# Attention block with sliding window and gated FFN on one core: values of eight heads in one stretch, probabilities kept per two heads

## The chip, the cores and the metric

The kernel runs on one core of one Trainium2 chip. The metric is device time in microseconds (us) of one execution; the figure that counts is the median over runs. Engines are called as in the profile: PE (matrix engine; PEld its weight loads), DVE (vector), ACT (scalar), POOL (GpSimd), SP (the queue that issues most transfers).

## The reference, cut to what matters

One transformer block over 2048 tokens of width 640, in fp32: layer norm, attention with 32 heads of 20 over a causal window of 256 tokens, residual, layer norm, gated FFN of width 1536, residual.

```python
qkv = layernorm(x) @ wqkv                      # 32 heads of 20
scores = q @ k.T * 20 ** -0.5                  # kept where 0 <= query - key < 256
o = softmax(scores) @ v @ wo
h = x + o
out = h + (gelu(layernorm(h) @ w_gate) * (layernorm(h) @ w_up)) @ w_down
```

## The kernel before, in words

The tokens are cut into 16 blocks of 128. A block's queries see their own block of keys and the two before it (`window`, L812), so blocks 0 and 1 see one and two, all others three. The dense products (q, k, v, output projection, FFN) are done as two fp16 halves per operand, three matmuls per product (`products`, L540).

Attention of one block has three kinds of PE work, each in a mode of the array of its own:

* **Maxima** (`maxima`, L834): for one pair of heads, q times k in row tiles (60 of 64 rows per head), into the PSUM tile `ra` or `rb` (two banks each, one per head of the pair). DVE then adds the mask and takes the row maximum with one `tensor_tensor_reduce` per head (`max_out`, L906). In the profile this is a `CUSTOM_DVE_ANT_0` row and a short `DVE_READ_ACCUMULATOR2_ANT` row that writes the maximum to `mxs`. The reduce also writes its elementwise result, which nobody reads; before, that goes to an SBUF tile `junk`, of which there is one.
* **Scores** (`scores`, L951): once all maxima of a block are known, they are put beside q as two more rows, and k times q in row tiles gives the transposed scores less the maximum, into the other of `ra` and `rb`. ACT takes the exponential into the SBUF tile `pt`, and POOL sets masked probabilities to zero with `affine_select`: two calls for the far edge of the window and one for the diagonal, and the diagonal alone in blocks 0 and 1 (`score_out`, L989).
* **Values** (`value_lane`, L1016): probabilities times v, four heads at a time in four column tiles, fp32, into `pv`. A unit of four heads is 4 matmuls per key block: 12 in most blocks, 24 records in the trace, since an fp32 matmul leaves two.

Dense matmuls and transposes use the whole array. After every second value group of eight heads ACT copies `pv` out, and the result is transposed and normalised.

**What sets the order.** The kernel is written as Python generators ("lanes"). A planner (`Clock`, `Engine`, and the loop at the end of `block_kernel`) prices each instruction with a small formula and issues the first lane whose inputs are ready by its own clock. The order that results is fixed at build time; each engine runs its list in order and waits on semaphores. The planner prices a change of array mode at 0.095 us (`SWITCH`), a DVE op on 320 elements at 0.065 + 0.00106 x 320 = 0.404 us, and a hop between engines at 0.18 us (`LAT`). If a tile's ring of buffers is full, the new tile counts as written when its predecessor's last use ends, and the hop is added (`tile`, L126): with its one buffer, `junk` makes each reduce start 0.18 us after the one before it, in the planner's clock.

`row_need` (L860) says when a maxima or scores stretch may start: its banks have to be free, and for scores a place in the ring of `pt` as well (three units of four heads). The loop tries values ahead of all else when PE is in row mode (`nc.mode == "row"`, L1633), so that a value stretch follows a row stretch where it can; when fewer than two units wait (`len(valq) < 2`, L1635) values aren't started from any other mode.

While nothing is ready and no score has been computed yet, the loop issues a 128-column matmul on `ident16` into `pv`, to keep PE going ("warmers" below).

Of the kernel before, what the change touches and what calls it, by code (L numbers as in the profile page):

```python
# [22 lines left out]
P = 128  # L23
# [230 lines left out]
def block_kernel(ctx: ExitStack, tc: tile.TileContext, x, wqkv, wo, wg, wu, wd, out):  # L254
# [85 lines left out]
    nc.vector.tensor_copy(ident16, ident)  # L340
    mhalf = const.tile([P, 1], F32, name="mhalf")
    nc.vector.memset(mhalf, -0.5)
    ones = const.tile([P, P], F32, name="ones")
    nc.vector.memset(ones, 1.0)


    NS = 16
# [229 lines left out]
    def ff_scales_down(fg):  # L577
# [15 lines left out]
    gu = gu.rearrange("p (a c f) -> p a c f", c=KC, f=512)  # L593

    HB = P // 2
    mask = wp.tile([P, 2 * P], F32, name="mask")
    nc.gpsimd.memset(mask, 0.0)
    nc.gpsimd.affine_select(mask[:, P:2 * P], mask[:, P:2 * P], pattern=[[-1, P]],
                            compare_op=ALU.is_ge, fill=NEG, base=0, channel_multiplier=1)
    band = wp.tile([P, 5 * HB], F32, name="band")  # L600
    nc.gpsimd.memset(band, 0.0)
    for a in range(2):
        first, last = band[HB * a:HB * a + HB, 0:HB], band[HB * a:HB * a + HB, 4 * HB:]
# [5 lines left out]
    maxq, tps, scoreq, valq, woq = [], [], deque(), deque(), deque()  # L609


    RV, RK = 5, 6
    vring = [wp.tile([P, H, DH + 1], F32, name=f"v{i}") for i in range(RV)]
    rooms["v"] = [v.rearrange("p h d -> p (h d)")[:, :D] for v in vring]
    kT = wp.tile([P, H // 2, RK, P], F16, name="kT")
# [97 lines left out]

    def load_x(j):
        if 0 < j < NR:
            t = at("pt", [P, 4, 3, P], F32, 3).rearrange("p a b c -> p (a b c)")
            B[j].x = t[:, 0:D]
        else:
            B[j].x = at("xt", [P, D], F32)
        nc.sync.dma_start(B[j].x, x[j * P:(j + 1) * P, :])  # L720
# [94 lines left out]
    def pairs(j):  # L815

        return 2 if j < 2 else 1
# [42 lines left out]
    def row_need():  # L860


        (ta, a), (tb, b_) = sorted((two(n), n) for n in ("ra", "rb"))
        tm, ts = [], []
        lead = pos["max"] - pos["score"]
        for j, pr in heapq.nsmallest(2, maxq) if lead < 2 * LEAD else ():
            b = B[j]
            tm.append(nc.ready((b.c.qT[0:60, pr, b.cols], kT[0:60, pr, j % RK, :],
                                b.c.qT[64:124, pr, b.cols], kT[64:124, pr, j % RK, :]),
                               "tensor"))  # L870
        free = 3 - (pos["units"] - pos["values"])
        for j, pr in list(scoreq)[:2]:
            b = B[j]
            free -= pr % 2 == 0
            if free >= 0:
                ts.append(nc.ready((b.c.qT[0:62, pr, b.cols], b.c.qT[64:126, pr, b.cols]),
                                   "tensor"))
        row.clear()
        late = max(ta, nc.t["tensor"]) + APART
        two_of = [(maxima, scores, tm[:1] + ts[:1]), (scores, scores, ts), (maxima, maxima, tm)]  # L880
        if lead > LEAD + SWAY:
            two_of = [two_of[1], two_of[0], two_of[2]]
        elif lead < LEAD - SWAY:
# [12 lines left out]
        return one[0][0]  # L896
# [9 lines left out]
    def max_out(j, pr, par, ps, at_):  # L906
        b = B[j]
        n = len(window(j))
        for k in range(pairs(j)):
            w = min(n * P, 5 * HB)  # L910
            head = ps[:, k * n * P:k * n * P + w]
            yield on("vector", head)
            junk = at("junk", [P, 5 * HB], BF16, 1)
            nc.vector.tensor_tensor_reduce(junk[:, :w], head,
                                           band if n == 3 else mask[:, (2 - n) * P:], 1.0,
                                           -3.0e38, ALU.add, ALU.max,
                                           b.mx[:, par * 16 + pr + k:par * 16 + pr + k + 1])
        done(at_)
        b.maxima += pairs(j)
        if b.maxima == H:  # L920
            tps.append(max_rows(j))
# [29 lines left out]
    def scores(at_):  # L951
        j, pr = scoreq.popleft()
        b = B[j]
        u = pr // 2
        if pr % 2 == 0:
            b.pt[u] = at("pt", [P, 4, 3, P], F32, 3)
            pos["units"] += 1
        n = len(window(j))
        t = bank(at_).rearrange("p (r c) -> p r c", r=2)
        for k in range(pairs(j)):  # L960
            if n == 3:
                steps = [((1, slice(0, 2), 1, 3),) * 2,
                         ((2, slice(0, 2), 3, 5), (0, slice(0, 2), 0, 6)),
                         ((0, slice(0, 1), 0, 1), (2, slice(1, 2), 4, 5))]
# [13 lines left out]
        t = t[:, :, :pairs(j) * n * P]  # L978
        tasks.append(score_out(j, pr, t, b.pt[u], at_))
        pos["score"] += pairs(j)  # L980

    def part(pt, n, i):
# [3 lines left out]
            return half[:, :, 2 * i:2 * i + 2]  # L986
        return (half[:, :, 0:6:5], half[:, :, 1:3], half[:, :, 3:5])[i]

    def score_out(j, pr, t, pt, at_):  # L989
        b = B[j]  # L990
        u = pr // 2
        n = len(window(j))
        m = pairs(j)
        yield on("scalar", t)
        w = min(n * P, 5 * HB)
        for k in range(m):
            h = 2 * (pr % 2 + k)
            nc.scalar.activation(pt[:, h:h + 2].rearrange("p h a b -> p h (a b)")[:, :, :w],
                                 t[:, :, k * n * P:k * n * P + w], AF.Exp, scale=esc)
        done(at_)  # L1000
        pos[j, u] += 2 * m
        if pos[j, u] < 4:
            return
        yield on("gpsimd", pt[:, :, 0, :])
        if n == 3:
            half = pt.rearrange("p h a (b c) -> p h (a b) c", b=2)
            for a, (i, o) in enumerate(((0, 0), (3, 5))):
                nc.gpsimd.affine_select(half[:, :, o], half[:, :, i], pattern=[[0, 4], [-1, HB]],
                                        compare_op=ALU.is_ge, fill=0.0, base=-1 - HB * a,
                                        channel_multiplier=1)  # L1010
        diag = part(pt, n, n - 1).rearrange("p h a b -> p h (a b)")
        nc.gpsimd.affine_select(diag, diag, pattern=[[0, 4], [1, P]],
                                compare_op=ALU.is_ge, fill=0.0, base=0, channel_multiplier=-1)
        valq.append((j, u))

    def value_lane():  # L1016

        while True:
            yield pe(when=lambda: valq and B[valq[0][0]].v == 2 and pos["ones"])
            j, u = valq.popleft()  # L1020
            b = B[j]
            pt = b.pt.pop(u)
            ks = window(j)
            n = len(ks)
            order = [1, 0, 2] if n == 3 else list(range(n))
            yield pe(pt, pv[:, u % 4, :])
            for k, i in enumerate(order):
                for c in range(4):
                    nc.tensor.matmul(pv[32 * c:32 * c + DH + 1, u % 4, :].rearrange(
                                         "p (a b) -> p a b", b=HB),  # L1030
                                     vring[ks[i] % RV][:, 4 * u + c, :], part(pt, n, i)[:, c],
                                     start=(k == 0), stop=(k == n - 1))
            pos["values"] += 1
# [665 lines left out]
```

## Time and profile before

| | |
|---|---|
| median of 3 runs | 1014.98 us (1014.44 to 1020.82) |
| the profiled execution, its own time | 1018.26 us |
| its span, first to last instruction | 1016.5 us |
| PE busy | 998.2 us (98%), 12925 matmul records |
| DVE busy | 749.2 us (74%) |
| ACT busy | 446.6 us (44%) |
| POOL busy | 313.2 us (31%) |
| granted PE clock | 1.00 throughout |

The attention part runs from the first maxima stretch at 52.4 us to about 583 us; after that PE does the FFN alone. Busy time of PE is modelled and overlaps, so the distance from one matmul's start to the next one's is the cost that counts; the timeline shows starts, and merges equal neighbours into one row with a count (x4, x12, x24). A "stretch" below is an unbroken run of matmuls of one kind.

### The profile page before, as it was taken

How to read it: one execution, taken by the hardware profiler on the slowest of the kernel's cores; microseconds unless marked ns; L12 is line 12 of the kernel's file. 1: busy time of each engine (PE TensorE's matmuls, PEld its weight loads, DVE VectorE, ACT ScalarE, POOL GpSimd, SP SyncE). 2: the span in 40 equal slices, each digit the busy share in tenths (PEclk: the TensorE clock that was granted, in tenths of full speed). 3: DMA queues.
4: the chain of work that ended last, by engine and by line, in shares of the span. 5: the costliest groups of instructions: out<-in, count | busy, mean ns of one | idle time of the engine just before them, and what ended most of it. 6: DMA issues, size and time to landing. Idle time of an engine off the chain costs nothing.

```text
span 1016.5 us, 30774 instructions
## 1 busy us (share of the span) xinstructions
PE 998.2 (98%) x12925; PEld 699.3 (69%) x12925; DVE 749.2 (74%) x2206; ACT 446.6 (44%) x721; POOL 313.2 (31%) x504
## 2 busy tenths in 40 slices
PE   8999999999999999999999999999999999999998
PEld 7876666766766676777655664567777777777776
DVE  5888898888867767775687687798888875544553
ACT  6514856755555555554657643432222222221220
POOL 7101544543433433332435411254313300000000
PEclk9999999999999999999999999999999999999999
DMA  8657587361441614127103433233553442222211
GB/s 308 131 121 170 156 165 203 83 148 39 114 113 54 119 53 108 43 67 191 36 29 106 93 118 104 78 130 111 143 188 94 144 153 78 79 99 84 79 53 52
DMA packets 105835, 112.68 MB, mean 111 GB/s; under 512 B 38368, under 2 KB 79584, under 8 KB 105696
## 3 DMA queue, kind: packets, MB, share of 16 engines
q1 hardware_dynamic: 93600, 99.97, 36.0%
q10 hardware_dynamic: 12096, 10.75, 3.4%
q8 instruction: 101, 1.65, 0.7%
q14 instruction: 38, 0.31, 0.1%
HBM read 73.73 MB, written 28.84 MB: 101 GB/s over the span
## 4 chain that ended last, share of the span: by engine, by line
PE 82%; DVE 7%; DMA 5%; ACT 3%; POOL 2%; issue 2%; SPq 0%; ACTq 0%; DVEq 0%; POOLq 0%
PE mm L199 41%; PE ra L199 12%; PE pv L199 11%; PE rb L199 10%; PE tp L199 7%; DVE junk L199 1%; DMA wsl<-in_wu_dram 1%; DMA kT<-qk 1%; DMA qk<-qks 1%; POOL pt L199 1%; DVE am L199 1%; DMA qT<-in_wqkv_dram 1%; ACT pt L199 1%; DVE ht L199 1%; POOL gu L199 0%
## 5 line engine op out<-in xcount | busy, mean ns | idle before, releaser
L199 POOL TENSOR_SCALAR_AFFINE_SELECT pt<-pt 128x512 f32<-128x512 f32 x352 | 174.4, 511 | 300.8 <-ACT pt L199 284.9
L199 DVE CUSTOM_DVE_ANT_0 junk<-ra,band 128x320 bf16<-128x320 f32 x238 | 116.4, 489 | 50.5 <-PE ra L199 45.1
L199 ACT ACTIVATE pt<-rb,esc 128x640 f32<-128x640 f32 (+2 forms) x135 | 102.4, 765 | 81.6 <-PE rb L199 61.1
L199 DVE CUSTOM_DVE_ANT_0 junk<-rb,band 128x320 bf16<-128x320 f32 x210 | 102.8, 489 | 35.0 <-PE rb L199 29.7
L199 ACT ACTIVATE pt<-ra,esc 128x640 f32<-128x640 f32 (+2 forms) x121 | 92.2, 769 | 67.3 <-PE ra L199 59.1
L199 PE MATMUL pv<-pt,v 128*21 128x128 f32 x2880 | 104.5, 275 | 1.2 <-issue 1.1
L199 PEld LDWEIGHTS <-ah 128*128 128x128 f16 x768 | 75.1, 98 | 28.5 <-issue 1.2
L199 ACT ACTIVATE gel<-gel,ffk 128x512 f32<-128x512 f32 x36 | 26.0, 721 | 135.6 <-DVE gel L199 135.6
L199 PEld LDWEIGHTS <-ws 128*128 128x128 f16 x720 | 70.4, 98 | 9.2 <-DVE ws L199 1.1
L199 PEld LDWEIGHTS pv<-pt,v 128*21 128x21 f32 x2880 | 68.5, 100 | 10.2 <-issue 0.8
L199 PEld LDWEIGHTS <-kT 62*64 62x64 f16 x2880 | 63.8, 106 | 11.9 <-issue 7.6
L199 PEld LDWEIGHTS <-qT 60*64 60x64 f16 x1280 | 30.2, 104 | 58.9 <-issue 50.8
L199 PEld LDWEIGHTS <-gu 128*128 128x128 f16 x440 | 41.8, 98 | 36.2 <-issue 2.1
L199 DVE SCALAR_TENSOR_TENSOR ht<-mm,ffk,ht 128x320 f32<-128x320 f32 x96 | 52.2, 545 | 13.9 <-PE mm L199 12.1
L199 ACT CAST ah<-gel 128x512 f16<-128x512 f32 x48 | 29.6, 617 | 70.6 <-DVE gel L199 70.4
L199 PE MATMUL mm<-xh,w1h 128*128 128x256 f16 x200 | 54.7, 273 | 0.9 <-DVE qks L199 0.9
L199 PE MATMUL mm<-xl,w1h 128*128 128x256 f16 x200 | 54.7, 273 | 0.0
L199 PE MATMUL mm<-xh,w1l 128*128 128x256 f16 x200 | 54.7, 273 | 0.0
L199 POOL TENSOR_TENSOR gelt<-gelt 128x256 f32<-128x256 f32 x18 | 15.5, 859 | 112.6 <-ACT gelt L199 112.6
L199 PE MATMUL mm<-w3h,ol 128*128 128x320 f16 x160 | 48.1, 301 | 0.0
L199 PE MATMUL mm<-w2h,xl 128*128 128x320 f16 x160 | 48.1, 300 | 0.0
L199 PE MATMUL mm<-w3h,oh 128*128 128x320 f16 x160 | 48.0, 300 | 0.0
(300 smaller groups left out, 2576.9 us busy)
## 6 DMA issues: line engine op xcount, KB each, us to landing
ws<-wsums SPq DMA_DIRECT2D x24, 640.0 KB
qk<-qks ACTq DMA_DIRECT2D x32, 256.0 KB
qT<-qk SPq DMA_DIRECT2D x48, 160.0 KB
kT<-qk SPq DMA_DIRECT2D x48, 160.0 KB
wsums<-ws SPq DMA_DIRECT2D x12, 640.0 KB
ht<-in_x_dram SPq DMA_DIRECT2D x16, 320.0 KB
h_dram<-ht SPq DMA_DIRECT2D x16, 320.0 KB
ht<-h_dram SPq DMA_DIRECT2D x16, 320.0 KB
```

What stands on the lines that cost most here:

```text
L199: r = real(*args, **kw)
```

## The change

Five edits, in `block_kernel` and the functions printed above:

1. `value_lane` takes two units (eight heads) at once: it waits until two are queued and all four of their probability tiles and both quarters of `pv` are ready, and issues both without a break.
2. `pt` becomes a ring of seven tiles of two heads, where it was three tiles of four heads. `row_need` counts in these.
3. POOL masks each two-head tile by itself: the same three calls (or one) on half as many elements, so twice as many calls.
4. The reduce for the maxima writes its unread elementwise result back over its own input in PSUM; `junk` is gone.
5. `mask` and `band` become bf16, and the unused tile `ones` is dropped, to make room in SBUF.

The diff, cut to its core:

```diff
-    ones = const.tile([P, P], F32, name="ones")
-    nc.vector.memset(ones, 1.0)
...
-    mask = wp.tile([P, 2 * P], F32, name="mask")
+    mask = wp.tile([P, 2 * P], BF16, name="mask")
...
-    band = wp.tile([P, 5 * HB], F32, name="band")
+    band = wp.tile([P, 5 * HB], BF16, name="band")
...
-    RV, RK = 5, 6
+    RV, RK, RP = 5, 6, 7
...
-        free = 3 - (pos["units"] - pos["values"])
+        free = RP - (pos["parts"] - 2 * pos["values"])
...
-            free -= pr % 2 == 0
+            free -= pairs(j)
...
-            junk = at("junk", [P, 5 * HB], BF16, 1)
-            nc.vector.tensor_tensor_reduce(junk[:, :w], head,
+            nc.vector.tensor_tensor_reduce(head, head,
                                            band if n == 3 else mask[:, (2 - n) * P:], 1.0,
...
-        u = pr // 2
-        if pr % 2 == 0:
-            b.pt[u] = at("pt", [P, 4, 3, P], F32, 3)
-            pos["units"] += 1
+        for k in range(pairs(j)):
+            b.pt[pr + k] = at("pt", [P, 2, 3, P], F32, RP)
+        pos["parts"] += pairs(j)
...
+        for k in range(pr, pr + pairs(j)):
+            pt = b.pt[k]
+            yield on("gpsimd", pt[:, :, 0, :])
+            if n == 3:
+                half = pt.rearrange("p h a (b c) -> p h (a b) c", b=2)
+                for a, (i, o) in enumerate(((0, 0), (3, 5))):
+                    nc.gpsimd.affine_select(half[:, :, o], half[:, :, i],
+                                            pattern=[[0, 2], [-1, HB]], compare_op=ALU.is_ge,
+                                            fill=0.0, base=-1 - HB * a, channel_multiplier=1)
...
+            pos[j, "u", k // 2] += 1
+            if pos[j, "u", k // 2] == 2:
+                valq.append((j, k // 2))
...
-            yield pe(when=lambda: valq and B[valq[0][0]].v == 2 and pos["ones"])
-            j, u = valq.popleft()
+            yield pe(when=lambda: len(valq) > 1 and B[valq[0][0]].v == 2 and pos["ones"])
+            j, u = valq[1]
...
-            yield pe(pt, pv[:, u % 4, :])
+            yield pe(*(b.pt[k] for k in range(2 * u - 2, 2 * u + 2)),
+                     pv[:, u % 4 - 1:u % 4 + 1, :])
+            for u in (u - 1, u):
+                valq.popleft()
+                pt = [b.pt.pop(k) for k in (2 * u, 2 * u + 1)]
```

The planner works the whole order out anew, so every engine's list changes. On PE, in the fourth block of tokens, the end of a scores stretch (`qT,kT`), a value unit (`pv<-pt,v`) and what follows stood so before:

```order
L199 LDWEIGHTS kT
L199 MATMUL rb<-qT,kT 64x64
L199 MATMUL pv<-pt,v_121 21x128 x4
L199 MATMUL pv<-pt,v_120 21x128 x4
L199 MATMUL pv<-pt,v_122 21x128 x4
L199 MATMUL tp<-ident,ht 128x128 x4
L199 LDWEIGHTS w0h
L199 MATMUL mm<-xh,w0h 128x256
```

and stand so now, a little further on (`kT,qT` is a maxima stretch, `mm` a dense product):

```order
L199 LDWEIGHTS kT
L199 MATMUL ra<-qT,kT 64x64
L199 LDWEIGHTS w0h
L199 MATMUL mm<-xh,w0h 128x256
L199 MATMUL pv<-pt,v_119 21x128 x4
L199 MATMUL pv<-pt,v_118 21x128 x4
L199 MATMUL pv<-pt,v_120 21x128 x4
L199 MATMUL pv<-pt,v_119 21x128 x4
L199 MATMUL pv<-pt,v_118 21x128 x4
L199 MATMUL pv<-pt,v_120 21x128 x4
L199 LDWEIGHTS qT
L199 MATMUL ra<-kT,qT 64x320
```

Two units now stand together, and they have moved from behind a row stretch to ahead of one. Over the whole list PE has 64 value stretches where it had 128, 247 row stretches where it had 258, and 568 runs of one array mode where it had 647; the number of matmuls of each kind is the same, but for 305 warmers where there were 328.

On DVE, among the maxima of the fourth block (`am<-wsl` takes the largest value of a slice of FFN weights, `ol<-tp,oh` is the low half of the attention output), the list read before:

```order
L199 ISA junk,mxs<-rb,band 128x320
L199 ISA mxs 128x1
L199 ISA junk,mxs<-rb,band 128x320
L199 ISA mxs 128x1
L199 TENSOR_TENSOR ol<-tp,oh 128x128
L199 ISA junk,mxs<-ra,band 128x320
```

and reads now:

```order
L199 ISA rb,mxs<-rb,band 128x320
L199 ISA mxs 128x1
L199 TENSOR_REDUCE am_2298<-wsl 128x1
L199 TENSOR_TENSOR ol<-tp,oh 128x512
L199 ISA ra,mxs<-ra,band 128x320
L199 ISA mxs 128x1
```

Each reduce now has `ra` or `rb` as output as well as input, and seven weight-slice reductions that used to come after the fourth block's last maximum have moved ahead of it.

On POOL, a unit's masking of three key blocks read before

```order
L199 AFFINE_SELECT pt_6534<-pt_6534 128x4x64 x2
L199 AFFINE_SELECT pt_6534<-pt_6534 128x4x128
L199 AFFINE_SELECT pt_6618<-pt_6618 128x4x64 x2
L199 AFFINE_SELECT pt_6618<-pt_6618 128x4x128
L199 AFFINE_SELECT pt_6703<-pt_6703 128x4x64 x2
```

and now

```order
L199 AFFINE_SELECT pt_5277<-pt_5277 128x2x64 x2
L199 AFFINE_SELECT pt_5277<-pt_5277 128x2x128
L199 AFFINE_SELECT pt_5312<-pt_5312 128x2x64 x2
L199 AFFINE_SELECT pt_5312<-pt_5312 128x2x128
L199 AFFINE_SELECT pt_5378<-pt_5378 128x2x64 x2
```

with half the elements per call and 704 calls in all where there were 352.

More of the change, by code (lines that the diff above doesn't have):

```diff
@@ L715, in load_x @@
         if 0 < j < NR:
-            t = at("pt", [P, 4, 3, P], F32, 3).rearrange("p a b c -> p (a b c)")
+            t = at("pt", [P, 2, 3, P], F32, RP).rearrange("p a b c -> p (a b c)")
             B[j].x = t[:, 0:D]
@@ L978, in scores @@
         t = t[:, :, :pairs(j) * n * P]
-        tasks.append(score_out(j, pr, t, b.pt[u], at_))
+        tasks.append(score_out(j, pr, t, at_))
         pos["score"] += pairs(j)
@@ L987, in part, with score_out @@
         return (half[:, :, 0:6:5], half[:, :, 1:3], half[:, :, 3:5])[i]
-    def score_out(j, pr, t, pt, at_):
+    def score_out(j, pr, t, at_):
         b = B[j]
-        u = pr // 2
         n = len(window(j))
-        m = pairs(j)
+        w = min(n * P, 5 * HB)
         yield on("scalar", t)
[L995 to L998, printed above, removed]
+        for k in range(pairs(j)):
+            nc.scalar.activation(b.pt[pr + k].rearrange("p h a b -> p h (a b)")[:, :, :w],
@@ L999, in score_out @@
                                  t[:, :, k * n * P:k * n * P + w], AF.Exp, scale=esc)
         done(at_)
[L1001 to L1014, printed above, removed]
+        for k in range(pr, pr + pairs(j)):
[7 more added lines that the diff above has]
+                                            fill=0.0, base=-1 - HB * a, channel_multiplier=1)
+            diag = part(pt, n, n - 1).rearrange("p h a b -> p h (a b)")
+            nc.gpsimd.affine_select(diag, diag, pattern=[[0, 2], [1, P]],
+                                    compare_op=ALU.is_ge, fill=0.0, base=0, channel_multiplier=-1)
+            pos[j, "u", k // 2] += 1
+            if pos[j, "u", k // 2] == 2:
+                valq.append((j, k // 2))
@@ L1016, in value_lane @@
     def value_lane():
         while True:
-            yield pe(when=lambda: valq and B[valq[0][0]].v == 2 and pos["ones"])
-            j, u = valq.popleft()
+            yield pe(when=lambda: len(valq) > 1 and B[valq[0][0]].v == 2 and pos["ones"])
+            j, u = valq[1]
             b = B[j]
-            pt = b.pt.pop(u)
             ks = window(j)
@@ L1025, in value_lane @@
             order = [1, 0, 2] if n == 3 else list(range(n))
-            yield pe(pt, pv[:, u % 4, :])
[L1027 to L1033, printed above, removed]
+            yield pe(*(b.pt[k] for k in range(2 * u - 2, 2 * u + 2)),
[3 more added lines that the diff above has]
+                pt = [b.pt.pop(k) for k in (2 * u, 2 * u + 1)]
+                for k, i in enumerate(order):
+                    for c in range(4):
+                        nc.tensor.matmul(pv[32 * c:32 * c + DH + 1, u % 4, :].rearrange(
+                                             "p (a b) -> p a b", b=HB),
+                                         vring[ks[i] % RV][:, 4 * u + c, :],
+                                         part(pt[c // 2], n, i)[:, c % 2],
+                                         start=(k == 0), stop=(k == n - 1))
+                pos["values"] += 1
             if u % 4 == 3:
```

## The prediction

> **What bounds the kernel now.** I read the page's first part and the chain of waits, then busy time by stretch, then who PE waited for, then timelines.
>
> ```profile
> span 1016.5 us, 30774 instructions
> PE 998.2 (98%) x12925; PEld 699.3 (69%) x12925; DVE 749.2 (74%) x2206; ACT 446.6 (44%) x721; POOL 313.2 (31%) x504
> PE 82%; DVE 7%; DMA 5%; ACT 3%; POOL 2%; issue 2%; SPq 0%; ACTq 0%; DVEq 0%; POOLq 0%
> ```
>
> PE carries 82% of the chain that ended last, so time is won on PE's list or not at all. Busy time by stretch tells two stages of attention apart; PE's waits (second fence, 47 to 200 us) say the same:
>
> ```profile
> 53.34:162.23 108.89, 105.98 (x1523) 74.35 (x1517) 95.59 (x374) 58.22 (x106) 33.65 (x47) 1.00 0.68 158
> 300.00:400.00 100.00, 99.83 (x1917) 70.00 (x1916) 74.17 (x271) 57.40 (x89) 39.01 (x83) 1.00 0.34 78
> ```
> ```profile
> PE ra L199 <- DVE mxs L199: 1.9, 2, 1.4
> PE tp L199 <- DVE ht L199: 1.6, 1, 1.6
> ```
>
> Between the first maximum and the fourth block's last (53.3 to 162.2 us) DVE (third of the busy times, behind PE and PEld) is busy 95.6 of 108.9 us and PE waits for it; later it has a quarter to spare and PE runs from one stretch into the next.
>
> **What the change takes from PE.** The price of a change of array mode stands in the timeline, as distances between starts:
>
> ```profile
> 111.54 0.27 PE L199 MATMUL mm<-xl,w0h 128*128 128x256 f16 x1
> 111.65 0.27 PE L199 MATMUL mm<-xh,w0l 128*128 128x256 f16 x1
> 111.85 0.33 PE L199 MATMUL ra<-kT,qT 60*64 60x320 f16 x4
> 112.01 0.40 PE L199 MATMUL rb<-qT,kT 62*64 62x128 f16 x16
> 112.33 0.64 PE L199 MATMUL pv<-pt,v 128*21 128x128 f32 x16
> 112.90 0.33 PE L199 MATMUL tp<-ident,o 128*128 128x128 f32 x1
> ```
> ```profile
> 402.93 0.30 PE L199 MATMUL mm<-w3l,oh 128*128 128x320 f16 x1
> 403.15 0.85 PE L199 MATMUL pv<-pt,v 128*21 128x128 f32 x24
> 403.94 0.31 PE L199 MATMUL mm<-w3h,ol 128*128 128x320 f16 x1
> 404.09 0.30 PE L199 MATMUL mm<-w3h,oh 128*128 128x320 f16 x1
> 404.22 0.30 PE L199 MATMUL mm<-w3l,oh 128*128 128x320 f16 x1
> 404.36 0.30 PE L199 MATMUL mm<-w3h,ol 128*128 128x320 f16 x1
> 404.59 0.33 PE L199 MATMUL rb<-kT,qT 60*64 60x320 f16 x4
> ```
>
> A dense matmul of 256 columns is followed by its like after 0.11 us and by a maximum after 0.20; one of 320 columns by its like after 0.14 and by a maximum or a value after 0.22 or 0.23. So a change of mode costs 0.09 us, whichever modes they are. PE's list has 79 fewer (647 to 568): 79 x 0.094 = **-7.4 us**. A value unit of 24 records lasts 403.15 to 403.94 = 0.79 us with the change behind it, one of 16 records 0.57, so 8 records cost 0.22. A double unit of 48 is then 0.79 + 3 x 0.22 = 1.44, where two apart are 1.57. Of the 0.13 saved 0.09 is the mode change already counted; the rest, 0.035 for each of 64 seams, is **-2.2 us**.
>
> ```profile
> L199 PE MATMUL pv<-ident 128*128 128x128 f16 x328 | 23.2, 230 | 2.5 <-DVE pv L199 2.5
> ```
>
> There are 23 fewer warmers at 23.2 / 328 = 0.07: **-1.6 us**, since other work stands where they stood. That is -11.2 on PE, all on the path as long as PE waits no longer than before. Nothing behind attention holds it back: the remaining FFN weights are scaled and split only once attention's buffers close, so that work moves with the end of attention.
>
> **What it gives back: the first four blocks.** Without `junk` the planner lets one reduce follow another 0.40 us apart (before: 0.58). The chip does this:
>
> ```profile
> 404.59 0.33 PE L199 MATMUL rb<-kT,qT 60*64 60x320 f16 x4
> ...
> 404.97 0.49 DVE L199 CUSTOM_DVE_ANT_0 junk<-rb,band 128x320 bf16<-128x320 f32 x1 [0.68 <-PE rb L199]
> ...
> 405.38 0.08 DVE L199 DVE_READ_ACCUMULATOR2_ANT mxs<- 128x1 f32 x1
> 405.50 0.49 DVE L199 CUSTOM_DVE_ANT_0 junk<-rb,band 128x320 bf16<-128x320 f32 x1
> ```
>
> Reduces start 0.53 apart, with a read of the accumulator between, which the planner doesn't price. It was cautious by 0.05 a reduce and becomes rash by 0.13, over 512 of them. It has therefore packed the maxima closer where there were many to do. Adding PE's rows by their distances, from the first maximum to the fourth block's last, gives 99.7 us in the old list and 87.6 in the new, because dense work was put off. DVE's list for the same stretch has not shrunk: seven weight reductions more (0.59 each), less some four other ops, is 3.9 us more. Before, 108.9 us went by here against PE's 99.7, so 9.2 of waits. Now DVE needs at least 95.6 + 3.9 = 99.5, and with all of its 13.3 us of idle time kept 112.8. PE's waits are thus 12 to 25, or 3 to 16 more. Part of the idle time was DVE waiting for maxima, which now queue ahead of it; I take 105 us, waits of 17.4: **+8 us**.
>
> **Later blocks, banks.** A bank comes free after 0.38 (maximum to first reduce) + 0.53 + 0.49 = 1.40, and with one hop 1.46 us; in the blocks whose maxima come in two runs of keys the hop to the first reduce is shorter, and it is 1.34:
>
> ```profile
> 249.16 0.33 PE L199 MATMUL rb<-kT,qT 60*64 60x256 f16 x8
> ...
> 249.55 0.49 DVE L199 CUSTOM_DVE_ANT_0 junk<-rb,band 128x320 bf16<-128x320 f32 x1
> ```
>
> I counted PE's work between a maximum and the next write to its bank, from the fifth block on. Before, none of 181 was under that; now 39 of 177 are, by 2.0 us in all: **+2 us**. Whether the reduce takes longer when it writes PSUM, no row shows; the nearest are fills:
>
> ```profile
> 1.67 0.17 DVE L199 MEMSET ones<- 128x128 f32 x1
> 1.71 0.06 DVE L199 MEMSET mhalf<- 128x1 f32 x1
> 1.94 0.48 DVE L199 MEMSET pv<- 128x512 f32 x1
> ```
>
> 0.06 for one element and 0.17 for 128 make 0.48 to 0.50 for 512, and the PSUM fill takes 0.48. So I price the new output at nothing. Below nothing there is no room, as the op still passes 320 elements; the upper bound is 0.07 a reduce, if the next op has to wait for the whole 0.49 of the row and not for the 0.42 after which it starts now.
>
> **Later blocks, probabilities.** A value stretch waits for ACT and POOL:
>
> ```profile
> 400.13 0.31 PE L199 MATMUL rb<-qT,kT 62*64 62x128 f16 x12
> 400.38 0.31 PE L199 MATMUL mm<-w2l,xh 128*128 128x320 f16 x1
> 400.50 0.79 ACT L199 ACTIVATE pt<-rb,esc 128x640 f32<-128x640 f32 x1
> 401.36 1.49 POOL L199 TENSOR_SCALAR_AFFINE_SELECT pt<-pt 128x256 f32<-128x256 f32 x3 [2.39 <-ACT pt L199]
> ```
> ```profile
> L199 POOL TENSOR_SCALAR_AFFINE_SELECT pt<-pt 128x256 f32<-128x256 f32 x224 | 91.1, 430 | 232.3 <-ACT pt L199 232.2
> L199 POOL TENSOR_SCALAR_AFFINE_SELECT pt<-pt 128x512 f32<-128x512 f32 x128 | 83.4, 651 | 68.5 <-ACT pt L199 52.7 <-issue 6.0 <-PE rb L199 2.1
> L199 POOL TENSOR_SCALAR_AFFINE_SELECT mask<-mask 128x128 f32<-128x128 f32 x1 | 0.3, 293 | 0.1
> ```
>
> From the row behind the scores to the end of masking is 402.85 - 400.38 = 2.47 us. Half a unit is two calls of 128 elements (0.29, from the mask's own row) and one of 256 (0.43): 1.01 for 1.49, so with a hop values may start 2.06 behind that row. The list leaves less in 28 of the 56 double stretches of three key blocks, by 1.2 us in all: **+1 us**. If halving a call saved nothing (0.43 each, the upper bound), it would be 12. POOL gets some 60 us more work, under idle time of 700. ACT's exponentials are the same, and the seven-tile ring leaves three tiles to fill while four are read.
>
> **The sum.** -7.4 - 2.2 - 1.6 + 8 + 2 + 1 = -0.2 us. That is 1016.3 against the profiled execution's span of 1016.5 (1018.26 in all); laid on the median of 1014.98, which is what the change will be measured by, **1014.8 us**. Its own range is 1009 to 1020.
>
> **Rivals.** (a) *The saving goes through whole.* If DVE's idle time in the first blocks collapses and the later gaps suffice, only 3 of waits is added: -11.2 + 3 = -8, **1007**. For it: PE's later waits are near nothing now, and a wait early in the list widens the gaps behind it. Against it: 99.5 us of DVE work doesn't fit under 87.6 of PE work. (b) *The in-place reduce is slower, and DVE becomes the bound; slower than before.* At 0.07 more a reduce, 128 of them add 9 us in the first four blocks, where DVE sets the pace, and the same count of gaps gives 5.5 in place of 2 later: -11.2 + 8 + 9 + 5.5 + 1 = +12.3, **1027**. One per cent is passed from 0.06 a reduce. Reduces 0.53 apart in 0.49-us rows speak for little slack, the fills against it. [...] (c) *Masks come late.* Values were started behind a row stretch and now start as soon as the planner thinks them ready. Were calls to cost 0.43 whatever their size: -11.2 + 8 + 2 + 12 = +11, **1026**; the 0.29 row of half the size speaks against it. That the merge fails to happen is ruled out by the list itself.
>
> **How the numbers follow.** Forecast 0.64, (a) 0.18, (b) 0.13, (c) 0.05. The range takes the forecast's and reaches toward (a) and (b): 1006 to 1024. One per cent, about what a measurement of this kernel tells from no change, is 10.1 us. Faster by more needs nearly all 11.2 with next to no waits, half of (a): 0.09. Slower by more is most of (b) and (c): 0.14. Within it: 0.77.
>
> **What would show it.** Right: 64 value stretches, double ones 1.44 us long; 0.09 us at a mode change; reduces 0.53 apart with PSUM as output; POOL calls of 0.29 and 0.43; more waits of PE for DVE before 165 us, with the fourth block's last maximum at about 159 us although less dense work is done by then; attention's end within a few us of 583. Wrong: reduces 0.6 apart (b); PE's value rows waiting for POOL (c); no more DVE waits than now in the first blocks, and attention over 8 us earlier (a).

## The result, and the profile after

The change takes 1029.86 us (median of 4 runs, 1027.69 to 1031.32) against 1017.5 for the kernel before (4 runs, one more than ahead of the prediction): ratio 1.0129, 95% interval 1.0107 to 1.0150. It is slower by 1.3%, outside the predicted range, and within 3 us of what rival (b) gave. The profiled execution took 1030.46 us.

The first part of the page of the change, and the engines' shares of the chain that ended last:

```profile
span 1028.7 us, 31190 instructions
PE 998.7 (97%) x12902; PEld 702.5 (68%) x12902; DVE 766.8 (75%) x2205; ACT 444.8 (43%) x721; POOL 375.0 (36%) x856
PE 69%; DVE 19%; DMA 4%; issue 4%; ACT 2%; POOL 1%; SPq 0%; ACTq 0%; DVEq 0%; POOLq 0%
```

The span grew by 12.2 us. PE's share of the chain fell from 82 to 69% and DVE's rose from 7 to 19%: PE now waits for DVE. DVE is 17.6 us busier with one instruction less, and the groups of instructions show where. First the kernel before, then the change (the last numbers of a row are busy us and mean ns of one, then idle time ahead):

```profile
L199 DVE CUSTOM_DVE_ANT_0 junk<-ra,band 128x320 bf16<-128x320 f32 x238 | 116.4, 489 | 50.5 <-PE ra L199 45.1
L199 DVE DVE_READ_ACCUMULATOR2_ANT mxs<- 128x1 f32 x512 | 42.3, 83 | 0.0
```
```profile
L199 DVE CUSTOM_DVE_ANT_0 ra<-ra,band 128x320 f32<-128x320 f32 x244 | 121.5, 498 | 41.9 <-PE ra L199 30.5 <-PE rb L199 6.8
L199 DVE DVE_READ_ACCUMULATOR2_ANT mxs<- 128x1 f32 x512 | 72.4, 141 | 0.0
```

The row of the reduce itself is hardly longer (498 ns for 489). What grew is the accumulator read behind it, 141 ns for 83: 58 ns, 512 times (neighbouring rows overlap, a read starting 0.42 us behind the start of a reduce of 0.49, so the groups' sums grow by more than the engine's busy time). A timeline of the change shows two reduces of one bank and the maximum that follows in it:

```profile
300.82 0.49 DVE L199 CUSTOM_DVE_ANT_0 rb<-rb,band 128x320 f32<-128x320 f32 x1
...
301.22 0.14 DVE L199 DVE_READ_ACCUMULATOR2_ANT mxs<- 128x1 f32 x1
...
301.40 0.50 DVE L199 CUSTOM_DVE_ANT_0 rb<-rb,band 128x320 f32<-128x320 f32 x1
...
301.82 0.14 DVE L199 DVE_READ_ACCUMULATOR2_ANT mxs<- 128x1 f32 x1
...
302.10 0.11 PEld L199 LDWEIGHTS <-qT 60*64 60x64 f16 x4 [0.26 <-DVE mxs L199]
302.10 0.33 PE L199 MATMUL rb<-kT,qT 60*64 60x320 f16 x4
```

Reduces start 0.58 apart here, 0.592 in the median over all (0.534 before). The read still starts 0.42 us behind its reduce (median), as before, so the 0.42 to 0.49 us that the prediction argued about is not where the time goes; the read ends later. The weight load for the next maximum then stands 0.26 us for it. Such waits are mostly put down to the weight load, so the waits of PEld have to be read beside those of PE. From 125 to 600 us, before and then the change (total us, times, longest):

```profile
PEld L199 <- DVE mxs L199: 0.3, 1, 0.3
PE ra L199 <- DVE mxs L199: 1.4, 1, 1.4
```
```profile
PEld L199 <- DVE mxs L199: 33.3, 98, 0.9
PE rb L199 <- DVE mxs L199: 1.8, 7, 0.7
PE ra L199 <- DVE mxs L199: 1.2, 6, 0.4
```

One such wait of a weight load has become 98. (The 33.3 us are no loss of that size: the 0.26 us above, up to 302.10, lie under the rows of two dense matmuls that start at 301.74 and 301.87 and last 0.30 each.) A double value unit lasts 336.66 to 338.10 = 1.44 us, and POOL's calls cost about what was forecast (0.29 and 0.43):

```profile
336.66 1.51 PE L199 MATMUL pv<-pt,v 128*21 128x128 f32 x48
338.10 0.33 PE L199 MATMUL rb<-kT,qT 60*64 60x320 f16 x4
```
```profile
L199 POOL TENSOR_SCALAR_AFFINE_SELECT pt<-pt 128x128 f32<-128x128 f32 x448 | 130.8, 316 | 193.1 <-ACT pt L199 192.8
L199 POOL TENSOR_SCALAR_AFFINE_SELECT pt<-pt 128x256 f32<-128x256 f32 x256 | 106.5, 418 | 28.1 <-ACT pt L199 12.5 <-PE mm L199 0.3
```

### The profile page after: what moved, and what is told of

The parts are those of the page before. It is cut to its first block, busy times and chain, and to the rows that moved or that the text cites. A ratio compares the mean times of both kernels' runs of the same rounds, so it can differ in the third digit from the quotient of the medians.

```text
span 1028.7 us, 31190 instructions
## 1 busy us (share of the span) xinstructions
PE 998.7 (97%) x12902; PEld 702.5 (68%) x12902; DVE 766.8 (75%) x2205; ACT 444.8 (43%) x721; POOL 375.0 (36%) x856
## 4 chain that ended last, share of the span: by engine, by line
PE 69%; DVE 19%; DMA 4%; issue 4%; ACT 2%; POOL 1%; SPq 0%; ACTq 0%; DVEq 0%; POOLq 0%
PE mm L199 31%; PE ra L199 11%; PE pv L199 11%; PE rb L199 9%; PE tp L199 7%; DVE ra L199 4%; DVE rb L199 4%; DMA qk<-qks 2%; DVE am L199 2%; DVE mxs L199 2%; DMA kT<-qk 1%; POOL pt L199 1%; DVE ht L199 1%; DVE qks L199 1%; DVE ts L199 1%
## 5 line engine op out<-in xcount | busy, mean ns | idle before, releaser
L199 POOL TENSOR_SCALAR_AFFINE_SELECT pt<-pt 128x128 f32<-128x128 f32 (+1 forms) x704 | 236.4, 353 | 221.2 <-ACT pt L199 205.3
L199 DVE CUSTOM_DVE_ANT_0 ra<-ra,band 128x320 f32<-128x320 f32 x244 | 121.5, 498 | 41.9 <-PE ra L199 30.5
L199 ACT ACTIVATE pt<-rb,esc 128x640 f32<-128x640 f32 (+2 forms) x140 | 105.6, 762 | 82.0 <-PE rb L199 68.7
L199 DVE CUSTOM_DVE_ANT_0 rb<-rb,band 128x320 f32<-128x320 f32 x204 | 101.5, 498 | 31.4 <-PE rb L199 19.5
L199 ACT ACTIVATE pt<-ra,esc 128x640 f32<-128x640 f32 (+2 forms) x116 | 89.2, 773 | 64.3 <-PE ra L199 45.9
L199 PE MATMUL pv<-pt,v 128*21 128x128 f32 x2880 | 92.5, 274 | 0.2
L199 PEld LDWEIGHTS pv<-pt,v 128*21 128x21 f32 x2880 | 73.8, 101 | 15.4 <-issue 13.2
L199 DVE DVE_READ_ACCUMULATOR2_ANT mxs<- 128x1 f32 x512 | 72.4, 141 | 0.0
L199 PEld LDWEIGHTS <-kT 62*64 62x64 f16 x2880 | 63.1, 106 | 11.2 <-issue 5.5
L199 POOL TENSOR_TENSOR rr<-rr 128x256 f32<-128x256 f32 x18 | 14.1, 783 | 105.5 <-ACT rr L199 105.5
L199 PE MATMUL ra<-kT,qT 60*64 60x320 f16 (+2 forms) x732 | 44.5, 278 | 5.1 <-DVE mxs L199 3.2
```

What stands on the lines that cost most here:

```text
L199: r = real(*args, **kw)
```

## The experiments

Three theories were to be told apart. **Length**: the reduce takes 0.058 us more with its output written over its input in PSUM, and that is what costs. **List**: the planner, which now charges 0.404 us for a reduce, makes an order that is too rash for any reduce (0.534 or 0.592). **Pairs**: merging the values costs PE the work that it had between maxima, whatever the reduces take. The rest is with the expectations.

To compare traces I use one reckoning for all. For each pair of PE rows that follow one another I take the median distance of their starts for that pair of forms over all the traces of the table (a value stretch counts as one row of its length). The sum of these medians is what a list would take without waits; what the distances exceed it by is lost, and is summed by stretch. The sum and the three losses shown fall some 10 us short of the span: 2.4 ahead of the first PE row, about 4 lost before 50 us, and the tail behind the last row's start. (The expectations of the later runs quote an earlier form of it with medians of each trace alone; the figures quoted differ by up to 5 us.)

| kernel | ratio to before [95%] | span | PE's rows without waits | lost 50-125 us | lost 125-600 us | lost behind |
|---|---|---|---|---|---|---|
| before | 1 | 1016.5 | 970.2 | 5.7 | 26.8 | 3.2 |
| the change | 1.0129 [1.0107, 1.0150] | 1028.7 | 959.6 | 14.5 | 41.0 | 3.6 |
| x1 its list, output in SBUF | 1.0041 [1.0022, 1.0060] | 1016.8 | 959.6 | 13.3 | 29.8 | 3.9 |
| x2 list of before, output in PSUM | 1.0007 [0.9988, 1.0027] | 1016.1 | 970.2 | 6.9 | 25.8 | 3.4 |
| x4 SBUF, charged as before | 1.0044 [1.0025, 1.0063] | 1020.0 | 970.6 | 4.7 | 25.2 | 9.4 |
| x5 in place alone | 1.0239 [1.0222, 1.0256] | 1036.3 | 966.4 | 14.3 | 42.8 | 3.0 |
| x7 single values, measured prices | 1.0103 [1.0081, 1.0125] | 1023.5 | 975.9 | 6.3 | 28.5 | 2.6 |
| x8 its list, half reduces | 0.9951 [0.9934, 0.9969] | 1009.8 | 959.6 | 12.6 | 23.2 | 4.4 |
| x9 SBUF, early blocks charged 0.534 | 0.9939 [0.9922, 0.9956] | 1007.3 | 960.9 | 8.3 | 25.0 | 3.1 |
| x10 PSUM, early blocks charged 0.599 | 1.0120 [1.0103, 1.0137] | 1028.1 | 965.3 | 7.0 | 43.2 | 2.8 |
| x11 SBUF, all charged 0.47 | 1.0072 [1.0053, 1.0090] | 1021.1 | 964.6 | 11.1 | 28.2 | 6.9 |
| x12 list of x9, output in PSUM | 1.0053 [1.0035, 1.0071] | 1017.6 | 960.9 | 7.8 | 35.1 | 4.0 |

(The two runs left out, x3 and x6, lose so much in one kind of stretch that their medians hold the waits.)

**x1, the change's list with the output in SBUF.** Every engine keeps its order; the unread output goes over memory that is not in use at that time.

```diff
-            nc.vector.tensor_tensor_reduce(head, head,
...
+            tc.nc.vector.tensor_tensor_reduce(junk[n][:, :w], head, m, 1.0, -3.0e38, ALU.add, ALU.max, top)
+            nc.issue("vector", nc.vector.cost("tensor_tensor_reduce", head, [head, m]), [head, m], [head, top])
```

(`tc.nc` isn't priced; the second line charges what the change was charged, so the planner decides alike.)

> PE's list and every other list of the change, instruction for instruction; only the unread elementwise output of the reduce goes to SBUF again (in blocks 2 to 15 over the mask of the first two blocks, which is dead by then, in blocks 0 and 1 over a dead input buffer). Theory A (the reduce with its output in PSUM holds DVE longer): the accumulator read falls from 141 ns to the 83 ns of before, two reduces follow each other 0.534 us apart and not 0.592, PE's waits for DVE shrink, and the time falls by 10 to 15 us to 1013 to 1019. Theory B (the planner's closer packing of the maxima does it, whatever the reduce costs): 0.534 us or not, the time stays within 4 us of the change, 1025 to 1031. Theory C (the bf16 masks make the reduce longer): the accumulator read stays at 141 ns, and so does the time.

1020.62 us: 9.2 less than the change, a little under the 10 to 15 that theory A gave, and 1.6 above its range. Its signs hold. The accumulator reads are back at 83 ns, although the masks are bf16 as in the change, two reduces follow 0.534 us apart, and the waits behind 125 us are fewer and sum to less:

```profile
L915 DVE DVE_READ_ACCUMULATOR2_ANT mxs<- 128x1 f32 x512 | 42.5, 83 | 0.0
```
```profile
PEld L199 <- DVE mxs L915: 24.3, 89, 1.1
```

Between the two lies nothing but the reduce's output: 9 us by the medians (1029.86 to 1020.62, with before at 1017.5 and 1016.83), and by the table, which compares one execution of each, 11.2 behind 125 us and 1.2 ahead. Some 3 of the 11.2 stand between 230 and 242 us: in the change's traced execution PE waits 2.1 us there for a load of keys (0.3 us in x1), and behind it the granted clock is at half for 3.4 us:

```profile
PE rb L199 <- DMA kT<-qk: 2.1, 1, 2.1
```
```profile
236.00:240.00 4.00, 3.92 (x40) 2.77 (x40) 2.96 (x10) 0.80 (x1) 1.15 (x3) 0.60 0.03 8
```

Whether the longer reduces made that load late isn't shown. The rest is spread over the whole stretch, about 1 us in 50.

Three things about the output change at once, though: it goes to PSUM and not to SBUF, it is fp32 and not bf16, and it lies over the reduce's own input. The reduce with its read grows by the same 57 to 58 ns at 128, 256 and 320 columns (334 to 391, 467 to 525 and 534 to 592 ns from one reduce to the next), so the growth is not one by the element; what a wider type alone would add isn't shown. No run changes one of the three alone, so "output in PSUM" below stands for all of them.

**x2, the list of before with the output in PSUM** (the call replaced in the same way, `junk` still charged, masks fp32).

> All lists of before, instruction for instruction, fp32 masks, values four heads at a time; only the unread output of the reduce goes over its input in PSUM. Theory A: the accumulator read takes 141 ns and reduces follow 0.592 us apart; DVE gets 512 x 0.058 = 30 us more, of which the 128 reduces of the first four blocks (7.4 us), where DVE sets the pace, are paid in full, and the later ones hardly, since the old list left no less than 1.56 us for a bank that now takes 1.52: 5 to 10 us slower than before, 1021 to 1027. Theory B: the old list has the room, within 2 us of before. Theory C: the accumulator read stays at 83 ns.

```profile
L916 DVE DVE_READ_ACCUMULATOR2_ANT mxs<- 128x1 f32 x512 | 72.5, 142 | 0.0
```
```profile
PEld L199 <- DVE mxs L916: 3.0, 12, 0.3
PEld tp L199 <- DVE mxs L916: 1.7, 8, 0.2
```

The read takes 142 ns with fp32 masks as well, so the output makes it and the masks don't. But the time, 1016.90 us, is that of before, as theory B had it. DVE does 18 us more work and PE hardly waits for it: a list made for reduces 0.58 us apart takes 0.592. So the length costs only where the list leaves no room for it, and length and list can't be priced apart.

**x3, the change with the reduce charged as measured,** and **x4, the output in SBUF and charged as before.**

```diff
+            if op == "tensor_tensor_reduce":
+                return 0.26 + 0.00104 * m
```

> The change as it is, output in PSUM, but the planner prices a reduce as measured (0.26 us + 1.04 ns an element, 0.592 for 320, where it had 0.404), so that it plans a list of its own: 535 runs of one array mode, 64 value stretches. Theory A with B (the lag of DVE behind the list is what costs): waits of PE for maxima fall to some 3 us, the merge's 9 to 11 us come through, less what DVE's 30 us of extra work costs the first blocks (0 to 8): 1006 to 1014. If instead DVE's extra work costs the same wherever the list puts it: 1022 or more.

> Value stretches of eight heads and the ring of seven as in the change, but the reduce writes SBUF and the planner charges the 0.18 us between reduces that the one junk buffer used to cost, so that it is cautious again: 562 runs of one mode, 64 value stretches. Theory A and B both: the merge's saving without the waits, 8.0 us from 85 mode changes and 2.2 from the seams, less 1 to 3 in waits for masks: 1006 to 1011. If merging itself costs (values waiting for POOL, the ring), then 1015 or more, with PE's value rows waiting for POOL.

Both missed: x3 takes 1047.06 us (ratio 1.0312, 1.0281 to 1.0343), x4 1021.96. The waits for maxima are gone, and others came. PE's waits in x3:

```profile
PE rb L199 <- ACT pt L199: 12.4, 14, 1.3
PE ra L199 <- ACT pt L199: 8.6, 10, 1.0
PE tp L199 <- DVE ws L199: 6.5, 1, 6.5
```

With dearer reduces the planner spends its dense work earlier: by the eighth block's last maximum PE has done 1363 dense matmuls in x3 and 1336 in x4, against 1181 in the change. Further on its list has stretches of 36 to 80 matmuls of scores and maxima with nothing between (8 in x3, 4 in x4, none over 24 in the change or before), and PE waits for ACT's exponentials, 21.0 us in all in x3 and 9.0 in x4. Busy time by stretch in x4, with PE first and the granted clock behind the five engines:

```profile
446.00:450.00 4.00, 2.82 (x71) 1.83 (x68) 3.82 (x16) 1.76 (x3) 2.45 (x8) 1.00 0.19 76
450.00:454.00 4.00, 2.43 (x89) 1.97 (x89) 2.19 (x9) 1.94 (x4) 2.06 (x7) 1.00 0.34 97
454.00:458.00 4.00, 2.41 (x64) 1.96 (x67) 2.58 (x12) 2.17 (x3) 2.34 (x8) 0.65 0.17 48
458.00:462.00 4.00, 4.00 (x60) 2.73 (x48) 1.57 (x6) 1.38 (x2) 1.49 (x6) 0.50 0.75 103
```

PE is 60 to 70% busy in the first three rows; in the third its clock falls to half, and it stays there for some seven us (455.2 to 462.0). x4 and x3 also have one wait of over 6 us in the FFN, for `ws`. So the price of a reduce moves more than the waits for reduces.

**x5, the output in place alone:** the call as the change writes it, the rest of the kernel as before.

> The kernel before with one part of the change alone: the reduce's unread output goes into the scores' bank (fp32 masks, values by one group, ring of three kept), and the planner orders the work anew by its own prices. The planner charges a reduce of 320 columns 0.404 us where it charged some 0.58 for the one with the ring of one unread tile; the change's trace shows a pitch of 0.592. Theory 'price' (a list made for reduces that are 0.19 us cheaper than they are makes TensorE wait for VectorE, whatever the values do): slower than before by 5 to 12 us, 1022 to 1029, waits of TensorE for the maxima of 5 us or more. Rival 'pairs' (only the paired values leave TensorE without other work while it waits): 1014 to 1020, waits for the maxima as before, under 2.5 us.

1040.3 us, far more than either theory gave, though in the direction of "price", and with its waits. From 125 to 600 us:

```profile
PEld L199 <- DVE mxs L199: 39.3, 126, 1.2
```

This speaks against "pairs": without paired values and their ring the same edit costs 2.4%, with them 1.3%. With the rest of the change the time is some 10 us lower, though on another list, so that isn't an exact price. It is the in-place output, with the lower price that the planner puts on it, that loses.

**x6, the change with reduces and POOL's calls charged as measured,** and **x7, the same with values by one group** (`len(valq) > 1` to `valq`, one group a turn).

```diff
-            return 0.46 if n == 1 else 0.06 + (0.00105 if op == "affine_select" else 0.00203) * n
+            return 0.46 if n == 1 else (0.17 + 0.00096 * n if op == "affine_select" else 0.06 + 0.00203 * n)
```

> The change with two prices of the planner set to what its trace shows: a reduce 0.26 + 1.04 ns per column (0.592 at 320), a GpSimd selection 0.17 + 0.96 ns per element (0.29 at 128, 0.42 at 256; the planner had 0.19 and 0.33). Theory 'price': the waits for maxima go, and with the selections charged rightly the waits for the probabilities seen in the runs with dearer reduces go too: 1008 to 1018. Rival 'pairs': with dearer engines around it the list has stretches of 40 to 80 matmuls of scores and maxima with nothing between (eight of them here, none in the change or before, four in the run that charged 0.58 for a reduce), since values wait until two groups are ready; each such stretch runs at the pace of ScalarE's exponentials and can end in a halved clock: 1030 to 1050.

> The same two prices, but the values by one group as before (halves of probabilities in a ring of seven and the output in the bank are kept). Rival 'pairs': most of the loss goes, three stretches of over 30 score matmuls are left: 1014 to 1024, at least 10 us under the paired run of the same prices. Theory 'price': one group costs the merged seams and mode changes again, 5 to 9 us more than the paired run of the same prices.

x6 takes 1052.3 us (ratio 1.0360, 1.0346 to 1.0375), x7 1025.42. The rival of "price" had both the right way, and each came out a little above what it gave. PE's waits for the exponentials in x6, then in x7:

```profile
PE rb L199 <- ACT pt L199: 12.3, 14, 1.3
PE ra L199 <- ACT pt L199: 10.1, 11, 1.5
```
```profile
PE rb L199 <- ACT pt L199: 2.7, 5, 1.0
PE ra L199 <- ACT pt L199: 2.6, 5, 1.0
```

Values held until two groups are ready are values that PE can't put between scores. With prices as measured, pairs cost 27 us; at the change's price they came, with the rest of the change, out 10 ahead (x5). Merging is no good or bad by itself: it depends on what else stands in the list.

**x8, the change's list with reduces of half the length** (x1 with every other column: `head[:, 0:w:2]`, 0.37 us by the pitch of its rows and 0.404 charged).

> The change's own list on every engine, with each reduce over every other column only (half of the keys are left out of each maximum) and its output in SBUF, so that a reduce takes about what the planner charged, 0.37 against 0.40 us. Theory 'price' (the list itself is worth what the prediction's gains say, 11 us, and all of it is lost to reduces that are longer than planned): 1004 to 1010, waits for maxima under 1 us. Rival (the merged values bring no gain in the time of the whole, whatever VectorE does): 1014 to 1020.

1011.97 us, between the two. Here DVE is as fast as the planner believed, and behind 125 us less is lost than before (23.2 to 26.8). The waits for maxima there are all but gone:

```profile
PEld L199 <- DVE mxs L915: 2.3, 6, 0.8
```

What is left is lost between 50 and 125 us, 12.6 us, where the change loses 14.5 and x1 13.3: shorter reduces win little back there. That stretch (PE's busy time first, DVE's third) in the change, then in x8, and PE's longest waits in it in x8:

```profile
50.00:125.00 75.00, 66.96 (x927) 47.29 (x925) 67.59 (x263) 35.44 (x67) 20.93 (x37) 1.00 0.69 167
```
```profile
50.00:125.00 75.00, 67.43 (x956) 48.77 (x955) 55.17 (x271) 37.53 (x70) 23.00 (x40) 1.00 0.76 170
```
```profile
PE mm L199 <- DVE qks L199: 1.8, 1, 1.8
PE tp L199 <- DVE am L199: 1.5, 1, 1.5
PE rb L199 <- DMA kT<-qk: 1.4, 1, 1.4
PE mm L199 <- ACT v L199: 1.2, 1, 1.2
```

**x9 to x11, charged in parts.** x9 charges 0.534 in blocks 0 to 3 and 0.404 behind, output in SBUF; x10 does it with 0.599 and the output in PSUM; x11 charges 0.47 in all blocks, output in SBUF.

```diff
+            nc.issue("vector", (0.195 if j < 4 else 0.065) + 0.00106 * w, [head, m], [top])
```

> The change with the reduce's unread output in SBUF (0.534 us a reduce of 320 columns, as in the first run), ordered anew with that 0.534 charged in the first four blocks and the change's 0.404 in the twelve behind. Runs so far: between 50 and 125 us TensorE loses 12 to 14 us in every list that was made at 0.404, and 5 to 7 in every list made at 0.58 or more, whatever the reduces take. Theory 'two places' (the early loss is the list's, the later one the reduce's length): the early loss falls to 5 to 7 us, the later one stays as in the first run at 26: 1011 to 1017. Rival (the gain is given back further on, as in the runs with dearer reduces throughout, through stretches of scores alone): 1019 or more, although the list has no such stretch over 24 matmuls.

> The change with its output in the bank as it is, ordered anew with 0.599 us charged for a reduce of 320 columns in the first four blocks and 0.404 behind. Theory 'two places': the early loss falls from 13.7 to 5 to 7 us and the later one stays at about 36: 1020 to 1025, slower than before still. Rival (the output in the bank costs only where VectorE is behind already, in the first four blocks): the later loss falls too, 1008 to 1016.

> The change with the unread output in SBUF, ordered anew with 0.47 us charged for a reduce of 320 columns in all blocks, between the change's 0.404 and the 0.534 that it takes. Theory 'two places': an early loss of about 9 us, half way between the lists at 0.404 and at 0.58, a later one under 26: 1014 to 1020. Rival (any replanning moves the time by several us up or down, so that a price says nothing): outside of that.

x9 came out as "two places" gave: 1011.02 us, 0.6% faster than before (interval 0.44 to 0.78%) and faster than the change, with an early loss of 8.3, a little over the 5 to 7 given (one wait of 3.0 us for `am` is part of it). x10 didn't: 1029.49 for 1020 to 1025. The early loss fell to 7.0, but behind it a load came late once, for 4.6 us, and the clock fell with it (last section). x11 took 1024.06, outside of its range, as its rival had it, with one wait of 2.5 us for `qks`, one of 3.3 for a transfer and one of 2.4 in the FFN. Most of these new lists have one to three such waits of their own, so a run with a new list tells less than one that keeps a list. Hence the last run.

**x12, the list of x9 with the output in PSUM:** the same on every engine.

> The list of the run that charged 0.534 us in the first four blocks only (SBUF output, 1011), the same on every engine, with the unread output put back into the scores' bank: a reduce takes 0.592 us again and nothing else differs. Theory 'length' (a list that charges 0.404 behind the fourth block cannot take the longer reduce, and its waits for maxima come back from 125 us on): the later loss rises from 23 to 30 to 36, time 1018 to 1026. Rival (the longer reduce costs time only in the first four blocks, where it is charged nearly in full here, and the run with its own list fell to one late load alone): 1009 to 1014.

1021.67 us against 1011.02, with before at 1016.1 and 1017.03, as "length" gave: on one list again, with the same one long wait in both (3.0 and 3.1 us, for `am`), the longer reduce costs 11 us, where it cost 9 from x1 to the change. PEld's waits from 125 to 600 us in x9, then in x12, and that stretch's busy times (PE first, DVE third) in the same order:

```profile
PEld L199 <- DVE mxs L915: 21.1, 81, 0.4
```
```profile
PEld L199 <- DVE mxs L915: 30.6, 88, 0.6
```
```profile
125.00:600.00 475.00, 471.85 (x8620) 327.84 (x8613) 367.56 (x1298) 276.18 (x434) 251.52 (x708) 1.00 0.41 100
```
```profile
125.00:600.00 475.00, 465.92 (x8557) 323.36 (x8556) 376.22 (x1271) 267.84 (x422) 245.88 (x706) 1.00 0.41 100
```

There are hardly more waits (88 for 81). On the mean each is longer, PE is 5.9 us less busy in the stretch, and all behind it is later. DVE idles 99 of these 475 us in x12: it is not short of time, only late for the next maximum.

## Why the prediction was wrong, point by point

**What PE saves (-11.2).** Right: -10.6 by the table (970.2 to 959.6). The price of a mode change, the double unit of 1.44 us and the seams hold together; they weren't measured one by one.

**The first four blocks (+8).** The size came out right by luck: 8.8 us more lost between 50 and 125 us, 7.6 of it also in x1, and the fourth block's last maximum at 160.2 us (158.6 in x1) where 159 was forecast. The reason was not right. I made DVE the bound; x8 takes 12 us of work from DVE in that stretch (67.59 us busy in the change, 55.17 in x8) and still loses 12.6 of the 14.5 us. There PE waits for single steps, since its dense work has been put off (665 dense matmuls by the fourth block's last maximum, 719 before). That they come late for that reason is argued, not shown; shown is that charging 0.534 in these blocks brings the loss to 8.3 (x9).

**Later blocks, banks (+2) and masks (+1).** With the reduce that I assumed (x1), 3.0 us more is lost behind 125 us than before, as added up. The way there differs: I had 39 gaps too short by 2.0 us in all, and x1 has 89 waits of weight loads for maxima. Value stretches hardly waited for POOL: the change has two such waits, 0.5 us in all, so rival (c) is out.

**The step that failed: "So I price the new output at nothing."** Measured is 0.058 us a reduce, in the accumulator read behind it, and with it the forecast's sign "reduces 0.53 apart with PSUM as output" failed. The fills that I took as evidence have no such read. In the traced executions the miss is what x1 and the change differ by: -10.6 + 7.6 + 3.0 is 0 for x1, where I had -0.2 and the spans differ by 0.3; adding 1.2 early and 11.2 later makes the change's 12.2 to within 0.2. About 3 of these stand around the one late load of keys and the halved clock behind it; most of the others stand between a dense matmul and a maximum behind it: there 9.4 us are lost behind 125 us in the change and 1.7 in x1, 9.0 in x12 and 0.7 in x9. By the medians the output makes 9 of the 12 us, and x1 itself stays 4 above before (below).

**Rival (b)** named this mechanism, gave 0.06 a reduce as the point where one per cent is passed, and a sum of +12.3. Its places were the wrong way round: it put 9 us in the first blocks and 3.5 behind them. The 5.5 us rested on a count of gaps under 1.40 us, 39 at the old length, where the change has 98 waits of weight loads for maxima; why the count came out too low isn't shown. I gave it 0.13, for a row without an accumulator read. The 58 ns were measured with the input in PSUM in all of these kernels, and the output's type and overlap are not told apart from its place.

**What stays open.** x1's timed median is 4 us over before's (1.0041), while their profiled executions differ by 0.3: x1's was among its fastest (1018.56 of 1016.77 to 1024.01), that of before, 1018.26, lies over its own median. The granted clock makes part of it. It comes and goes from execution to execution: of x1's twelve, five had a mean clock of 1.000 and took 1016.77 to 1018.85, and seven had 0.997 to 0.999 and took 1020.23 to 1024.01; of the 29 of before, 21 had 1.000 (median 1015.55) and eight less (median 1020.02). Among those at 1.000 x1 is still 3.0 us over before, and what makes these 3 stays open.

## What to carry to other kernels

An output that nobody reads is still written somewhere, and here that had a price of 58 ns a reduce: look for an instruction of the same kind, its accumulator read included, before pricing it at nothing. Where a planner writes the order, an edit that changes what it charges changes two things at once; keep the list and change the instruction (x1, x2, x12), or keep the instruction and change the price, before judging either. And an engine that idles a fifth of its time (99 of 475 us in x12) can still set the pace, if its results are wanted 0.06 us before they are there.

## What the runs showed of the hardware

**The accumulator read.** It lasts 83 ns behind a reduce that writes bf16 to SBUF and 141 behind one that writes fp32 over its input in PSUM, whatever the mask's type (83 in before and x1, 141 in the change and 142 in x2) and at 128, 256 and 320 columns alike; the reduce's own row (489 and 498 ns at 320 columns) hides it.

**The halved clock.** In x10 a wait of PE was paid more than once. PE waits 4.56 us for keys; ahead of it dense matmuls start 0.14 us apart, behind it 0.27, and the granted clock is 0.50:

```profile
300.60 0.30 PE L199 MATMUL mm<-w3h,ol 128*128 128x320 f16 x1
300.74 0.30 PE L199 MATMUL mm<-w3h,oh 128*128 128x320 f16 x1
...
308.65 0.48 PE L199 MATMUL ra<-kT,qT 60*64 60x320 f16 x3 [4.56 <-DMA kT<-qk]
...
310.10 0.47 PE L199 MATMUL mm<-w3h,oh 128*128 128x320 f16 x1
310.37 0.47 PE L199 MATMUL mm<-w3l,oh 128*128 128x320 f16 x1
```
```profile
308.00:312.00 4.00, 3.35 (x26) 2.04 (x26) 1.12 (x4) 0.80 (x1) 0.95 (x3) 0.50 0.01 4
312.00:316.00 4.00, 4.00 (x58) 2.39 (x60) 1.85 (x6) 0.92 (x2) 0.95 (x3) 0.74 0.17 66
```

From 300 to 325 us 8 us are lost for a wait of 4.6; the clock is at half for some seven. The clock fell behind shorter waits too. The change's 2.10 us were followed by 3.4 us at half clock; x11, with its three waits of 2.4, 2.5 and 3.3 us, ran at a mean clock of 0.994; and in x9 and x12, with one wait of 3.0 and 3.1 us between 50 and 125 us, the clock of that stretch was 0.98. Single waits of 1.5 us in x2, 1.6 in before and 1.8 in x8 left it at 1.00. And in x4 the clock fell to half at 455.2 us, behind eight us (446 to 454) in which PE was 66% busy, among scores and maxima, and no wait of PE from 440 to 460 us was over 1.3 us: a thin stretch stood ahead of it, and no long wait.
